# Gated mix of linear attention and expert lookup: output matmuls in a queue, the last tile's scores early, and a new end

## The chip, the core and the metric

The kernel runs on one core of one Trainium2 chip. The metric is device time of one execution in microseconds. A core has five engines that work side by side, each through its own list of instructions in order: TensorE (PE) multiplies matrices into PSUM, VectorE (DVE) and ScalarE (ACT) read and write PSUM and SBUF, GpSimd (POOL) works on SBUF alone, and SyncE (SP) here only issues DMAs. PSUM has eight banks of 512 floats per partition.

## What is computed

The input x has 2048 rows of 512. Two results are mixed by a gate g = sigmoid(x · gate_w): out = g · a + (1 − g) · b.

```python
# a: linear attention with 32 heads of 16
q, k, v = split(x @ wqkv)
phi(t) = concat(softmax(t @ w_phi), softmax(-(t @ w_phi)))
kv, z  = phi(k)^T v,  sum over rows of phi(k)
a      = ((phi(q) kv) / (phi(q) z + 1e-6)) @ wo

# b: 32 heads, each picks one of 16 x 16 experts
s1, s2 = (x w_q)[first half] k1^T, (x w_q)[second half] k2^T
e      = argmax(s1) * 16 + argmax(s2)          # K = 1, so the softmax over K is 1
b      = sum over heads of gelu(x . u[e]) * v[e]
```

Since K is 1, b depends only on how many of the 32 heads pick each expert: b = (count · gelu(x u^T)) v. The count is made with bit operations.

## The kernel before

Rows are cut into 16 tiles of 128. Most products are made in three matmuls per 128 rows of the contraction: every operand is split into a high part (`xh`, `wbh`, `ch`) and a low part (`xl`, `wbl`, `cl`), and high·high, high·low and low·high are added up in one PSUM bank.

The first 130 us form the weights, k, v and the sum kv over all tiles (in the bank `kvacc`). The second part, which the change is about, goes through the tiles again. Its order is written out by hand: the body of a Python loop over `a`, and an end behind it, call helpers, and the order of the calls is the order of the instructions on each engine. Nothing reorders them. In iteration `a` several tiles are under way: n = a+1, a, b = a−1 and z = a−2. The helpers, in the order of one tile's life:

- `front_s(t, half)`: scores of one half, 12 matmuls into a bank `s`. `front_p(t)`: x u^T and the gate, 12 matmuls of 258 columns into `pp`. `best(t, half)` on DVE: maximum and `is_equal` into `eq`. `turn_eq(t)`: a transposing DMA on SP's queue, `eq` to `et`. `gelu_pre(t)` on ACT: what GELU and gate need from `pp`.
- `front_q(t)`: 12 matmuls into `pq`. `soft_in(t)` on DVE: two reductions and two subtractions (`d`); between them stand steps of the count of tile t−1. `soft_exp` on ACT, `soft_w` on POOL (`w`), `soft_sum`, `soft_y`, `soft_p` and `soft_b` on DVE and POOL: the normalised features, again in `d`.
- `mid_mask(t)`: 16 small instructions on PE, `et` to the bank `mk`. `count(t)`: a generator of 18 DVE steps that makes `C`, the count per expert, from `mk`; `step` takes one step, `drain` the rest. Its scratch tiles `sa`, `sb` exist twice, for even and odd t.
- `planes(t)`, `join(t)`: transposition of `d` by ACT copies and two transposing DMAs into `pt`; `mid_phi(t)` does the same with PE transposes and two ACT evictions, without a DMA. `mid_num(t)`: 32 short matmuls into two banks `oT`, ACT writes their high part (`xh`, whose tile is no longer needed), `num_lo(t)` the low part on DVE (`xl`).
- `coef(t)`: count times gelu. `c_planes`, `c_join`, `back_cl`: its transposition by DMA into `ch`, `cl`; `back_c` does it with PE (bank `CT`).
- `back(t)`: 18 output matmuls of 512 columns into one bank `po`: 12 with the attention part (`back_o`, `back_ol`, which want `xh`, `xl`) and 6 with the expert part (`back_out`, which want `ch`, `cl`). `store(t)`: an ACT copy and a DMA.

Four PSUM banks (`mm`) are used in turn by `s`, `pp`, `pq` and `po`, three (`tr`) by `mk`, `oT` and `pt`; `kvacc` has the eighth. In iterations 2 to 9 `back` works on tile z. Iteration 10 makes no output at all (`defer = 10`), and from 11 on `back` is one tile further behind.

Of the kernel before, what the change touches and what calls it, by code (L numbers as in the profile page):

```python
# [20 lines left out]
P = 128  # L21
# [13 lines left out]
def mix_kernel(ctx, tc, xT, wqT, wkT, wv, wphi, wo, wq, kk, ug, ev, cst, out):  # L35
# [6 lines left out]
    def mm_bank(name):  # L42
        return psum.tile([P, 512], F32, tag="mm", bufs=4, name=name)
# [407 lines left out]
    def soft_y(t, i):  # L451
        e = st8[t]
        dve.tensor_reduce(pair(e["st"][:, 224:288])[:, :, 1 - i], hs(e["w"], i), axis=AX.X, op=ALU.add)
# [84 lines left out]
    def mid_mask(t):  # L538
        e = st8[t]
        o = tr_bank(f"mk{t}")[:, :64]  # L540
        for half in range(2):
            for w in range(2):
                for q in range(2):
                    pe.matmul(o[:, half * 32 + w * F:half * 32 + w * F + F], e["et"][:, half * 4 + w * 2 + q, :],
                              wm[:, q, :], start=(q == 0), stop=(q == 1))
        chains[t] = count(t, o)

    def count(t, o):
        e = st8[t]
        A, B = sa[t % 2], sb[t % 2]  # L550
        bor = ALU.bitwise_or
        yield dve.tensor_copy(A[:, :, 8:24], o.rearrange("p (g a) -> p g a", a=F))
        yield dve.tensor_tensor(B[:, :, 8:24], A[:, :, 8:24], A[:, :, 7:23], op=bor)
# [8 lines left out]
        yield dve.tensor_tensor(m2.rearrange("p (w a) -> p w a", a=F), A[:, 2:4, 8:24], A[:, 2:4, 7:23],  # L562
                                op=ALU.bitwise_xor)
# [18 lines left out]
        e["C"] = w3.tile([P, NX], F32, tag="cf", name=f"cf{t}")  # L582
        x8 = X[:, :NX].bitcast(U8).rearrange("p (n b) -> p n b", b=2)
        yield dve.tensor_tensor(e["C"], x8[:, :, 0], x8[:, :, 1], op=ALU.add)

    def coef(t):
        e = st8[t]
        (pool if t < NT - 2 else dve).tensor_tensor(e["C"], e["C"], e["G"], op=ALU.mult)

    def c_planes(t):  # L590
        e = st8[t]
# [26 lines left out]
        ch, cl, o = st8[t]["c"]  # L618
        eng.tensor_tensor(cl, o[:, :2 * P], ch, op=ALU.subtract)

    def back_o(t):
        e = st8[t]
        po = e["po"] = mm_bank(f"po{t}")
        oh, ol, _ = e["o"]
        for k in range(NK):
            pe.matmul(po, oh[:, k, :], wbh[:, k, :], start=(k == 0), stop=False)  # L626
            pe.matmul(po, oh[:, k, :], wbl[:, k, :], start=False, stop=False)  # L627

    def back_ol(t):
        po, (_, ol, _) = st8[t]["po"], st8[t]["o"]  # L630
        for k in range(NK):
            pe.matmul(po, ol[:, k, :], wbh[:, k, :], start=False, stop=False)  # L632

    def back_out(t):
        e = st8[t]
        po = e["po"]
        ch, cl, _ = e["c"]
        for j in range(2):
            js = slice(j * P, (j + 1) * P)
            pe.matmul(po, ch[:, js], eh[:, j, :], start=False, stop=False)  # L640
            pe.matmul(po, ch[:, js], el[:, j, :], start=False, stop=False)  # L641
        for j in range(2):
            pe.matmul(po, cl[:, j * P:(j + 1) * P], eh[:, j, :], start=False, stop=(j == 1))  # L643

    def store(t):
        po = st8.pop(t)["po"]
        ot = w3.tile([P, D], F32, tag="ot", name=f"ot{t}")
        if t < NT - 1:
            act.copy(ot, po)
            sp.dma_start(out[t * P:(t + 1) * P, :], ot)  # L650
        else:
            for i, q in enumerate((sp, act)):
                cols = slice(256 * i, 256 * i + 256)
                (act.copy if i else dve.tensor_copy)(ot[:, cols], po[:, cols])
                q.dma_start(out[t * P:(t + 1) * P, cols], ot[:, cols])
# [59 lines left out]
    def back(t):  # L715
        back_o(t)
        back_ol(t)
        back_out(t)
        store(t)

    defer = 10
    for a in range(NT - 1):
        n, b, z = a + 1, a - 1, a - 2
        y = z if a < defer else -1 if a == defer else z - 1
        B, Z = b >= 0, z >= 0
        if Z:
            mid_num(z)
# [44 lines left out]
        front_s(n, 1)  # L772
        front_p(n, False)
# [34 lines left out]
    back_cl(z, pool)
    num_lo(z)
    for _ in gate(a):  # L810
        step(b)
    step(b, 4)
    soft_in(a)
    soft_exp(a)
    gelu_act(a)
    back(z - 1)
    mid_mask(a)
    soft_w(a)
    gelu_out(a)
# [81 lines left out]
```

## Time and profile before

| | |
|---|---|
| median of 3 runs | 382.03 us (381.43 to 384.12) |
| the profiled execution | 381.71 us, of which its span is 379.9 us |
| PE busy | 367.2 us (97%) |
| DVE busy | 319.9 us (84%) |
| ACT, POOL busy | 236.3 us (62%), 161.3 us (42%) |
| clock of TensorE that was granted | 1.000 |
| second pass over the tiles, from pq of tile 0 | 128.6 us to the end |

Times in the rows below are microseconds from the start of the span; in a timeline row the first number is the start, the second the duration, then engine, line, operation, output, inputs, shapes and count. In the chain of waits each row is one piece of the chain that ended last. Matmuls overlap, so what one costs is the distance to the next start, not its duration. A busy PE is therefore not idle, but it may wait inside for its weights.

### The profile page before, as it was taken

How to read it: one execution, taken by the hardware profiler on the slowest of the kernel's cores; microseconds unless marked ns; L12 is line 12 of the kernel's file. 1: busy time of each engine (PE TensorE's matmuls, PEld its weight loads, DVE VectorE, ACT ScalarE, POOL GpSimd, SP SyncE). 2: the span in 40 equal slices, each digit the busy share in tenths (PEclk: the TensorE clock that was granted, in tenths of full speed). 3: DMA queues.
4: the chain of work that ended last, by engine and by line, in shares of the span. 5: the costliest groups of instructions: out<-in, count | busy, mean ns of one | idle time of the engine just before them, and what ended most of it. 6: DMA issues, size and time to landing. Idle time of an engine off the chain costs nothing.

```text
span 379.9 us, 9164 instructions
## 1 busy us (share of the span) xinstructions
PE 367.2 (97%) x3655; PEld 292.9 (77%) x3655; DVE 319.9 (84%) x785; ACT 236.3 (62%) x416; POOL 161.3 (42%) x170
## 2 busy tenths in 40 slices
PE   7999999999999999999999999999979999999983
PEld 3777687787768888788888888888867878888862
DVE  4459967766868889889999999999999999999993
ACT  4245466546638355869669669668667678678430
POOL 2105445325324733945436436427426436436500
PEclk9999999999999999999999999999999999999999
DMA  7469795596694034254343342342540441441201
GB/s 268 165 239 342 185 288 214 127 272 226 172 307 106 3 85 83 81 74 97 62 95 82 72 97 72 83 98 58 97 98 14 111 99 44 110 90 49 57 31 55
DMA packets 72220, 46.66 MB, mean 123 GB/s; under 512 B 63728, under 2 KB 64496, under 8 KB 69872
## 3 DMA queue, kind: packets, MB, share of 16 engines
q1 hardware_dynamic: 71312, 45.24, 45.2%
q10 hardware_dynamic: 864, 0.82, 0.8%
q8 instruction: 29, 0.48, 0.5%
q14 instruction: 15, 0.12, 0.1%
HBM read 26.39 MB, written 4.19 MB: 80 GB/s over the span
## 4 chain that ended last, share of the span: by engine, by line
PE 45%; DVE 12%; POOL 2%; ACT 2%; issue 1%; ACTq 0%; DVEq 0%
PE s L61 5%; PE s L60 5%; PE s L59 4%; PE pq L61 3%; PE pq L60 3%; PE po L626 3%; PE po L627 3%; PE po L632 3%; PE pq L59 2%; PE oT L525 2%; PE s L57 2%; PE po L640 2%; PE po L643 1%; PE pq L57 1%; PE po L641 1%; PE pp L60 1%
## 5 line engine op out<-in xcount | busy, mean ns | idle before, releaser
L439 POOL TENSOR_TENSOR w<-d,zb 128x512 f32<-128x512 f32 x32 | 40.8, 1296 | 85.3 <-ACT d L433 82.9
L200 POOL TENSOR_TENSOR d<-d,st 128x1024 f32<-128x1024 f32 x16 | 31.1, 1941 | 68.0 <-DVE st L199 58.1
L61 PE MATMUL s<-sh,xl 128*128 128x480 f32 x128 | 48.6, 380 | 0.0
L60 PE MATMUL s<-sl,xh 128*128 128x480 f32 x128 | 48.5, 379 | 0.0
L433 ACT ACTIVATE d<-d 128x512 f32<-128x512 f32 x32 | 20.1, 631 | 45.5 <-DVE d L109 36.8
L474 POOL TENSOR_TENSOR d<-d,st 128x512 f32<-128x512 f32 x30 | 31.2, 1062 | 27.9 <-DVE st L468 25.6
L516 ACT COPY pt<-tp 128x1024 uint16<-128x1024 uint16 x28 | 36.5, 1375 | 0.1
L59 PE MATMUL s<-sh,xh 128*128 128x480 f32 x96 | 36.3, 378 | 0.0
L353 ACT ACTIVATE d<-d 128x1024 f32<-128x1024 f32 x16 | 17.0, 1064 | 26.8 <-DVE d L111 26.7
L506 ACT COPY pl<-d 128x1024 uint16<-128x1024 uint16 x28 | 29.2, 1045 | 5.9 <-POOL d L474 5.9
L61 PEld LDWEIGHTS s<-sh,xl 128*128 128x128 f32 x128 | 24.0, 188 | 4.1
L60 PEld LDWEIGHTS s<-sl,xh 128*128 128x128 f32 x128 | 24.1, 188 | 3.4
L626 PE MATMUL po<-wbh,xh 128*128 128x512 f32 x64 | 25.3, 395 | 0.0
L627 PE MATMUL po<-wbl,xh 128*128 128x512 f32 x64 | 25.1, 392 | 0.0
L198 DVE TENSOR_REDUCE st<-d 128x64 f32<-128x1024 f32 x16 | 19.5, 1219 | 6.4 <-ACT d L353 6.1
L61 PE MATMUL pk<-wah,xl 128*128 128x480 f32 x64 | 24.4, 380 | 0.0
L60 PE MATMUL pk<-wal,xh 128*128 128x480 f32 x64 | 24.3, 380 | 0.0
L60 PE MATMUL pq<-wal,xh 128*128 128x480 f32 x64 | 24.3, 379 | 0.0
L61 PE MATMUL pq<-wah,xl 128*128 128x480 f32 x64 | 24.2, 379 | 0.0
L61 PE MATMUL pv<-wbh,xl 128*128 128x512 f32 x60 | 23.6, 394 | 0.0
L60 PE MATMUL pv<-wbl,xh 128*128 128x512 f32 x60 | 23.5, 392 | 0.0
L483 DVE TENSOR_TENSOR eq<-s,mx 128x512 bf16<-128x512 f32 x32 | 22.1, 692 | 1.2
(176 smaller groups left out, 1053.4 us busy)
## 6 DMA issues: line engine op xcount, KB each, us to landing
wq<-wq SPq DMA_DIRECT2D x16, 1024.0 KB, 5.8
xr<-xT SPq DMA_DIRECT2D x15, 256.0 KB, 6.1
y<-ot SPq DMA_DIRECT2D x15, 256.0 KB, 2.0
rawk<-wkT SPq DMA_DIRECT2D x1, 1024.0 KB, 6.9
rawq<-wqT SPq DMA_DIRECT2D x1, 1024.0 KB, 5.0
rawo<-wo SPq DMA_DIRECT2D x4, 256.0 KB, 3.6
rawu<-ug SPq DMA_DIRECT2D x2, 258.0 KB, 6.3
rawv<-wv ACTq DMA_DIRECT2D x2, 256.0 KB, 4.8
```

Of the source, the lines that this page charges most:

```text
L59: pe.matmul(o_, ah, bh[:, r], start=False, stop=False)
L60: pe.matmul(o_, ah, bl[:, r], start=False, stop=False)
L61: pe.matmul(o_, al, bh[:, r], start=False, stop=(last and i == n - 1))
L200: pool.tensor_tensor(g64(d), g64(d), b64(st[:, 128:192]), op=ALU.mult)
L433: act.activation(hs(d, i), hs(d, i), AF.Exp)
L439: pool.tensor_tensor(hs(e["w"], i), hs(e["ph"], i), hs(zb, i), op=ALU.mult)
L474: eng.tensor_tensor(g64(d)[:, gs_], g64(d)[:, gs_], r[:, gs_].unsqueeze(2).to_broadcast([P, 32, F]), op=ALU.mult)
L483: dve.tensor_tensor(e["eq"][:, 512 * half:512 * half + 512].rearrange("p (h f) -> p h f", f=F), p3, mx.unsqueeze(2).to_broadcast([P, H, F] ...
L506: act.copy(pl, e["ph"][:, halves[i]].bitcast(U16).rearrange("p (c j) -> p j c", j=2))
L516: act.copy(p16[:, :, 4 * i:4 * i + 4, :], e["tp"][i].rearrange("p (j g) n -> p j g n", j=2))
L626: pe.matmul(po, oh[:, k, :], wbh[:, k, :], start=(k == 0), stop=False)
L627: pe.matmul(po, oh[:, k, :], wbl[:, k, :], start=False, stop=False)
```

## The change

Five things are changed.

1. **Output matmuls in a queue.** `push(t)` appends the 18 output matmuls of tile t to a list, `pop(n)` issues the next n. Iteration `a` pushes tile z and pops 17 for a = 3 to 12, else 18, so that one more matmul is left in the list after each of these ten iterations. Even tiles accumulate in the bank of `kvacc`, odd ones in one of the four. `store_ended` copies and stores the tiles whose last matmul was issued. No iteration goes without output matmuls any more.
2. **Tile 15 early.** Scores, `best`, the transposing DMA, the mask and the whole count of tile 15 are made in iteration 1, with a third pair of scratch tiles and a count tile of its own. The mask of tile 1 moves ahead of the scores there. `kv_final` moves ahead of `join(0)`.
3. **The loop ends at iteration 13.** Tiles 14 and 15 have a new end, in which `pp` of tile 15 is made beside tile 14.
4. **In the end**, the features of tile 13 are joined before the exponentials of tile 14; the expert coefficients of tiles 13 and 15 are transposed by DMA, those of tile 14 by PE; `coef` of tile 15 is on POOL.
5. **The output of tile 15** goes into two banks of 256 columns, each with its own 18 matmuls, copy and DMA: expert part first, attention part last.

```diff
 def count(t, o):
-        A, B = sa[t % 2], sb[t % 2]
+        i = 2 if t == NT - 1 else t % 2
+        A, B = sa[i], sb[i]
...
+    def push(t):
+        e, h = st8[t], {}
+        def mm(lhs, rhs, first=False, last=False):
+            def go():
+                if first:
+                    h["po"] = e["po"] = (psum.tile([P, 512], F32, tag="acc", name=f"po{t}") if t % 2 == 0 else
+                                         mm_bank(f"po{t}"))
+                pe.matmul(h["po"], lhs(), rhs, start=first, stop=last)
+                if last:
+                    ended.append(t)
+            return go
...
+    def pop(n):
+        for _ in range(n):
+            queue.pop(0)()
...
-    for a in range(NT - 1):
+    last = NT - 1
+    for a in range(NT - 2):
...
-        if y >= 0:
-            back(y)
-        if a > 1:
+        if Z:
+            push(z)
+            pop(17 if 2 < a < 13 else 18)
+            store_ended()
+        if a > 0:
             mid_mask(a)
...
+        if a == 1:
+            front_s(last, 0)
+            front_s(last, 1)
         if a == 1:
-            mid_mask(a)
             kvacc(NT - 2)
             kvacc(NT - 1)
...
+            best(last, 0)
...
+        if a == 1:
+            best(last, 1)
+            turn_eq(last)
+            front_s(n, 1, range(2))
+            mid_mask(last)
+            front_s(n, 1, range(2, NK))
+            front_p(n, False)
+            kv_final()
...
+        if a == 1:
+            for l in (sa, sb):
+                dve.memset(l[2], 0)
+            drain(last)
...
+    a, b, z = NT - 2, NT - 3, NT - 4
...
+    soft_in(a, dealt(a, b, z))
+    drain(b)
+    gelu_act(a)
+    join(b)
+    push(z)
+    pop(10)
+    mid_mask(a)
+    pop(len(queue))
+    soft_exp(a)
+    store_ended()
+    mid_num(b)
+    front_q(last)
+    soft_w(a)
...
+    gelu_in(last)
+    push(b)
+    pop(12)
+    soft_in(last)
+    soft_exp(last)
+    mid_phi(a)
+    soft_w(last)
+    c_join(b)
+    back_cl(b, pool)
...
+    pop(4)
+    mid_num(a)
+    pop(2)
+    store_ended()
+    num_lo(a)
+    soft_y(last, 0)
...
+    push(a)
+    pop(12)
+    mid_phi(last)
+    c_join(last)
+    back_cl(last, pool)
+    drain(a)
+    coef(a)
...
+    last_c(last, pA, cA)
+    mid_num(last)
+    last_c(last, pB, cB)
+    num_lo(last)
+    back_c(a)
+    back_cl(a)
+    last_o(last, pA, cA)
...
+    pop(6)
+    store_ended()
+    last_o(last, pB, cB)
```

DVE between iterations 1 and 2, before (`sa1`, `sb1` belong to the count of tile 1, `mx1_2` and `eq2` to the best of tile 2, `oT0_0` and `oT1_0` to tile 0, `pq2` to tile 2):

```order
L555 TENSOR_TENSOR sb1_83<-sa1_81 128x4x16
L468 SCALAR_TENSOR_TENSOR st21_1916<-st21_1916,gs1_1857 128x32 x2
L556 TENSOR_TENSOR sa1_81<-sb1_83 128x4x16
L482 TENSOR_REDUCE mx1_2_2112<-s1_2_2039 128x32
L483 TENSOR_TENSOR eq2_2076<-s1_2_2039,mx1_2_2112 128x512
L536 TENSOR_TENSOR xl_62<-oT0_0_2125,xh_61 128x256
L536 TENSOR_TENSOR xl_62<-oT1_0_2126,xh_61 128x256
L105 TENSOR_REDUCE st22_2175<-pq2_2158 128x32
```

The same place after the change; `X15`, `T15` and `cf15` belong to the count of tile 15:

```order
L578 TENSOR_TENSOR X15_2182<-X15_2182,T15_2183 128x512
L579 TENSOR_TENSOR T15_2183<-X15_2182 128x256
L580 TENSOR_SCALAR X15_2182<-T15_2183 128x128
L581 TENSOR_SCALAR T15_2183<-T15_2183 128x128
L582 TENSOR_TENSOR X15_2182<-X15_2182,T15_2183 128x256
L586 TENSOR_TENSOR cf15_2194<-X15_2182 128x256
L536 TENSOR_TENSOR xl_62<-oT0_0_2196,xh_61 128x256
L536 TENSOR_TENSOR xl_62<-oT1_0_2197,xh_61 128x256
L105 TENSOR_REDUCE st22_2246<-pq2_2229 128x32
L397 RECIPROCAL gs2_2163<-gs2_2163 128x1
```

Between the best of tile 2 and the low part of tile 0's result (`xl`) now stands the whole count of tile 15, of which these are the last six steps.

ACT in the end, before, from the join of tile 13's coefficients on (`pt14` are the evictions of tile 14's transposes, `d215` the exponentials of tile 15):

```order
L600 COPY ctj13_4671<-tpc13_4624 128x2x256
L604 CAST ch13_4673<-ctj13_4671 128x256
L499 COPY pt14_4689<-pt0_14_4690 128x512
L499 COPY pt14_4689<-pt1_14_4696 128x512
L433 ACTIVATE d215_4718<-d215_4718 128x32x16 x2
L405 ACTIVATE gs15_4643<-gs15_4643 128x1
```

The same instructions after the change:

```order
L433 ACTIVATE d215_4759<-d215_4759 128x32x16 x2
L499 COPY pt14_4767<-pt0_14_4768 128x512
L499 COPY pt14_4767<-pt1_14_4774 128x512
L602 COPY ctj13_4783<-tpc13_4720 128x2x256
L606 CAST ch13_4785<-ctj13_4783 128x256
L405 ACTIVATE gs15_4734<-gs15_4734 128x1
```

The exponentials of tile 15 have moved from behind `ch13` and `pt14` to ahead of both.

More of the change, by code (lines that the diff above doesn't have):

```diff
@@ L581, in count @@
         yield dve.tensor_tensor(X[:, :NX], X[:, :NX], T[:, :NX], op=ALU.add)
-        e["C"] = w3.tile([P, NX], F32, tag="cf", name=f"cf{t}")
+        e["C"] = (w4.tile([P, NX], F32, tag="cfl", bufs=1, name=f"cf{t}") if t == NT - 1 else
+                  w3.tile([P, NX], F32, tag="cf", name=f"cf{t}"))
         x8 = X[:, :NX].bitcast(U8).rearrange("p (n b) -> p n b", b=2)
@@ L587, in coef @@
         e = st8[t]
-        (pool if t < NT - 2 else dve).tensor_tensor(e["C"], e["C"], e["G"], op=ALU.mult)
+        (dve if t == NT - 2 else pool).tensor_tensor(e["C"], e["C"], e["G"], op=ALU.mult)
     def c_planes(t):
@@ L619, in back_cl @@
         eng.tensor_tensor(cl, o[:, :2 * P], ch, op=ALU.subtract)
[L621 to L624, printed above, removed]
+    queue, ended = [], []
+    def push(t):
[9 more added lines that the diff above has]
+            return go
@@ L625, in back_o @@
         for k in range(NK):
[L626 to L630, printed above, removed]
+            queue.append(mm(lambda k=k: e["o"][0][:, k, :], wbh[:, k, :], first=k == 0))
+            queue.append(mm(lambda k=k: e["o"][0][:, k, :], wbl[:, k, :]))
         for k in range(NK):
-            pe.matmul(po, ol[:, k, :], wbh[:, k, :], start=False, stop=False)
@@ L634, in back_out @@
[L634 to L637, printed above, removed]
+            queue.append(mm(lambda k=k: e["o"][1][:, k, :], wbh[:, k, :]))
+        part = lambda i, j: lambda: e["c"][i][:, j * P:(j + 1) * P]
+        for j in range(2):
+            queue.append(mm(part(0, j), eh[:, j, :]))
+            queue.append(mm(part(0, j), el[:, j, :]))
+        for j in range(2):
+            queue.append(mm(part(1, j), eh[:, j, :], last=j == 1))
+    def pop(n):
+        for _ in range(n):
+            queue.pop(0)()
@@ L638, in back_out, with store_ended, last_c @@
+    def store_ended():
+        for t in ended:
+            ot = w3.tile([P, D], F32, tag="ot", name=f"ot{t}")
+            act.copy(ot, st8.pop(t)["po"])
+            sp.dma_start(out[t * P:(t + 1) * P, :], ot)
+        ended.clear()
+    def last_c(t, po, cols):
+        ch, cl, _ = st8[t]["c"]
         for j in range(2):
             js = slice(j * P, (j + 1) * P)
-            pe.matmul(po, ch[:, js], eh[:, j, :], start=False, stop=False)
-            pe.matmul(po, ch[:, js], el[:, j, :], start=False, stop=False)
+            pe.matmul(po, ch[:, js], eh[:, j, cols], start=(j == 0), stop=False)
+            pe.matmul(po, ch[:, js], el[:, j, cols], start=False, stop=False)
@@ L642, in back_out @@
         for j in range(2):
[L643 to L655, printed above, removed]
+            pe.matmul(po, cl[:, j * P:(j + 1) * P], eh[:, j, cols], start=False, stop=False)
@@ L657, in kv_final, with last_o @@
+    def last_o(t, po, cols):
+        oh, ol, _ = st8[t]["o"]
+        for k in range(NK):
+            pe.matmul(po, oh[:, k, :], wbh[:, k, cols], start=False, stop=False)
+            pe.matmul(po, oh[:, k, :], wbl[:, k, cols], start=False, stop=False)
+        for k in range(NK):
+            pe.matmul(po, ol[:, k, :], wbh[:, k, cols], start=False, stop=(k == NK - 1))
     def kv_final():
@@ L771, in mix_kernel @@
             w4 = ctx.enter_context(tc_pool("w4", "right"))
-        front_s(n, 1)
-        front_p(n, False)
+            for l in (sa, sb):
+                l.append(w4.tile([P, 4, 24], U16, tag=f"s{len(sa)}{len(sb)}", bufs=1, name=f"s{len(sa)}{len(sb)}"))
+        if a > 0:
+            front_s(n, 0)
+        if a != 1:
+            front_s(n, 1)
+            front_p(n, False)
         soft_w(a)
@@ L780, in mix_kernel @@
             wo_load((2, 3))
-        best(n, 0)
+            best(last, 0)
+        else:
+            best(n, 0)
         soft_y(a, 0)
         soft_y(a, 1)
+        if a == 1:
[4 more added lines that the diff above has]
+            front_s(n, 1, range(2, NK))
+            front_p(n, False)
+            kv_final()
         soft_p(a)
@@ L790, in mix_kernel @@
         if a == 1:
-            kv_final()
             for k in range(2, NK):
@@ L797, in mix_kernel @@
                 pool.tensor_tensor(wbl[:, k, :], rawo[k], wbh[:, k, :], op=ALU.subtract)
+            best(n, 0)
         best(n, 1)
@@ L800, in mix_kernel @@
         gelu_pre(n)
-    a, b, z = NT - 1, NT - 2, NT - 3
+        if a == 1:
+            for l in (sa, sb):
+                dve.memset(l[2], 0)
+            drain(last)
+    a, b, z = NT - 2, NT - 3, NT - 4
     mid_num(z)
+    planes(b, 0)
     c_join(z)
+    planes(b, 1)
     front_q(a)
-    mid_phi(b)
+    front_p(last, False)
     gelu_in(a)
-    gelu_out(b)
[L808 to L819, printed above, removed]
+    num_lo(z)
+    soft_in(a, dealt(a, b, z))
[11 more added lines that the diff above has]
+    soft_w(a)
+    gelu_out(b)
+    coef(b)
     soft_sum(a, 0)
     soft_sum(a, 1)
-    mid_num(b)
-    back(z)
     soft_y(a, 0)
-    step(a)
     soft_y(a, 1)
     soft_p(a)
-    soft_b(a, lambda t: None)
+    c_planes(b)
@@ L829, in mix_kernel @@
+    soft_b(a)
+    gelu_pre(last)
     num_lo(b)
-    back_o(b)
-    mid_phi(a)
-    back_ol(b)
-    drain(b)
-    coef(b)
+    for _ in gate(last):
+        pass
+    gelu_in(last)
[3 more added lines that the diff above has]
+    soft_exp(last)
+    mid_phi(a)
+    soft_w(last)
+    c_join(b)
+    back_cl(b, pool)
+    gelu_act(last)
+    gelu_out(last)
+    coef(last)
+    soft_sum(last, 0)
+    soft_sum(last, 1)
+    pop(4)
     mid_num(a)
-    back_c(b)
+    pop(2)
+    store_ended()
     num_lo(a)
-    back_cl(b)
@@ L839, in mix_kernel @@
-    back_out(b)
-    store(b)
+    soft_y(last, 0)
+    soft_y(last, 1)
+    gelu_out(a)
+    c_planes(last)
+    soft_p(last)
+    soft_b(last, lambda t: None)
+    push(a)
[3 more added lines that the diff above has]
+    back_cl(last, pool)
     drain(a)
     coef(a)
-    back_o(a)
-    back_ol(a)
+    poA, poB = mm_bank("poA"), mm_bank("poB")
+    pA, pB = poA[:, :256], poB[:, :256]
+    cA, cB = slice(0, 256), slice(256, 512)
+    last_c(last, pA, cA)
+    mid_num(last)
+    last_c(last, pB, cB)
@@ L845, in mix_kernel @@
+    num_lo(last)
     back_c(a)
     back_cl(a)
-    back_out(a)
-    store(a)
+    last_o(last, pA, cA)
+    ot = w3.tile([P, D], F32, tag="ot", name=f"ot{last}")
+    act.copy(ot[:, cA], pA)
+    sp.dma_start(out[last * P:, cA], ot[:, cA])
+    pop(6)
+    store_ended()
+    last_o(last, pB, cB)
+    otB = w3.tile([P, D], F32, tag="ot", name=f"otB{last}")
+    act.copy(otB[:, cB], pB)
+    act.dma_start(out[last * P:, cB], otB[:, cB])
 def _consts():
```

9 lines of the change are left out of this document (removed).

## The prediction

> **What bounds the kernel now.** I read TensorE's (PE's) own waits first, then the chain of work that ended last, and the timelines around the two places that the change touches. PE's waits (waiter, what released it, us in total, times, longest):
>
> ```profile
> PE CT L611 <- DVE cf L588: 2.4, 2, 1.7
> PE mk L544 <- DMA et<-eq: 2.0, 1, 2.0
> ...
> PE po L640 <- ACT ch L614: 1.0, 2, 0.5
> ...
> PE oT L525 <- ACT kvb L660: 0.8, 1, 0.8
> PE oT L525 <- ACT pt L516: 0.6, 1, 0.6
> ```
>
> From the first tile iteration on, PE idles 6.8 us and no more. 3.4 of it (CT, po) lies at the very end, 2.6 (mk, pt) in iteration 10, where the old kernel leaves one tile's output out, and 0.8 in front of iteration 2. Everything else is PE after PE. One steady iteration in the chain that ended last (start, us, what), with the VectorE (DVE) rows that follow:
>
> ```profile
> 319.48 0.43 PE pq L57
> 322.30 0.23 PE po L626
> ...
> 326.66 0.33 PE s L57
> 333.47 0.60 PE oT L525 x32
> 334.06 0.43 PE pq L57
> 336.92 0.69 DVE st L105
> ...
> 339.47 0.33 DVE cl L619
> ...
> 341.92 0.60 DVE d L109
> ```
>
> An iteration is 14.58 us of PE: pq 2.8, the 18 output matmuls and the mask 4.4 (0.23 for one matmul), scores and pp 6.8, oT 0.6. DVE's own round is in its timeline:
>
> ```profile
> 322.42 0.68 DVE L105 TENSOR_REDUCE st<-pq 128x32 f32<-128x512 f32 x1
> ...
> 336.06 0.75 DVE L536 TENSOR_TENSOR xl<-oT,xh 128x256 fp32r<-128x256 f32 x2
> ```
>
> From pq's first reduction to the end of xl it works without a gap for 13.6 + 0.7 = 14.3 us, then waits 0.2 for the next pq (336.92). The two engines are almost equally loaded: work that is moved from one place to another is free only where it meets an idle.
>
> **Part 1: tile 15's scores, mask and count in iteration 1.** Rows of the old iteration 1, on PE and on DVE:
>
> ```profile
> 149.64 0.40 PE L57 MATMUL s<-sh,xh 128*128 128x512 f32 x1
> ...
> 152.25 0.36 PE L544 MATMUL mk<-wm,et 128*128 128x16 bf16 x8
> 152.54 1.30 PE L207 MATMUL kvacc<-v,d 128*32 128x16 f32 x128
> 153.77 0.50 PE L57 MATMUL s<-sh,xh 128*128 128x512 f32 x1
> ...
> 158.84 1.21 PE L525 MATMUL oT<-pt,kvb 64*32 64x128 f32 x32 [0.78 <-ACT kvb L660]
> ```
> ```profile
> 152.96 0.68 DVE L482 TENSOR_REDUCE mx<-s 128x32 f32<-128x512 f32 x1
> 153.67 0.69 DVE L483 TENSOR_TENSOR eq<-s,mx 128x512 bf16<-128x512 f32 x1
> 154.28 1.27 DVE L453 TENSOR_REDUCE st<-w 128x32 f32<-128x512 f32 x2
> ```
>
> PE: half a score is 149.64 to 152.25, 2.6; mask 0.3; kvacc 1.2. In the new order PE does from 149.64 mask 0.3, scores of 15 5.2, kvacc 1.2, scores of 2 5.2, mask of 15 0.3, pp 1.6: oT can start at 163.4, 4.6 later than 158.84. There the old kernel waited for kvb and ran oT 0.6 longer than in the chain's row; in the new order the kvb copies stand before the join and are long done, so the 0.6 goes: **+4.0** at pq of tile 2, which ends at 163.4 + 0.6 + 2.8 = 166.8. Moved DMAs: the transpose of tile 15's eq goes into SP's queue here, behind two loads of wo; its mask stands six matmuls into s1 of tile 2, and I take it as covered (it costs up to 1 if the transpose is late).
>
> DVE: best of tile 15 is two halves of 1.3 (152.96 to 154.28), and the count is what the old tail shows it to be when nothing is woven into it:
>
> ```profile
> 367.76 0.19 DVE L553 TENSOR_TENSOR sb<-sa 128x64 uint16<-128x64 uint16 x1
> ...
> 372.55 0.42 DVE L584 TENSOR_TENSOR cf<-X 128x256 f32<-128x256 uint8 x1
> ```
>
> That is 5.2 us, 5.6 with the cast and two small memsets. From 152.96: 1.3, sums 1.2, 1.3, the softmax chain 1.5 to 2.2, so about 158.7; then DVE waits for s1 of tile 2, which PE ends at 161.9, best 1.3 (163.4), count 5.6: 169.0. Only behind it stand the low part of o (xl, 0.7) and, 2.9 after pq's first reduction started, cl (336.92 to 339.47 + 0.33): cl of tile 0 is there at 172.6. PE needs it at the 17th output matmul, 166.8 + 16 x 0.23 = 170.5. **+2.0**, a wait of the whole PE queue (mask, scores of tile 3, everything behind), and no later slack gives it back. Its bounds: 0, if DVE's steps are quicker than alone, up to 5.3 by the next rows, POOL and DVE side by side:
>
> ```profile
> 145.34 0.74 POOL L401 TENSOR_TENSOR x<-x,px 128x256 f32<-128x256 f32 x1
> ```
> ```profile
> 145.38 0.73 DVE L562 TENSOR_TENSOR m<-sa 128x32 uint16<-128x32 uint16 x1
> ```
>
> The count's small step started with POOL's product and ended with it: 0.73 for a 32-column step. By the Trainium skill, "SBUF — State Buffer", section "Who interferes with whom", a DVE instruction with two SBUF inputs and a GpSimd instruction that reads SBUF hold a shared port against each other, each for its whole length. The trace agrees in this row, and the rule speaks against moving the count next to POOL's work; by it the sum would go to the slow rival below if POOL's long subtractions were still running.
>
> **Part 2: one matmul put off in each of iterations 3 to 12.** 10 x 0.23 = **-2.3**; DVE's 14.3 just fits under the 14.35 that is left. The old kernel leaves a tile out in iteration 10, and the new one does not. That stretch (from:to, its length, then busy us of PE, PE's loads, DVE, ACT, POOL, clock, DMA):
>
> ```profile
> 276.68:290.02 13.34, 10.82 (x97) 8.75 (x89) 12.59 (x34) 9.22 (x17) 6.74 (x7) 1.00 0.35 70
> ```
>
> 13.34 (10.82 of PE, so 2.5 idle) against 14.58: **+1.2**. The second PSUM bank for the even tiles costs nothing: the four rotating banks are then used by four tiles instead of five. Sum up to pq of tile 14: 4.0 + 2.0 - 2.3 + 1.2 = +4.9, so it starts at 334.06 + 4.9 = 339.0.
>
> **Part 3: the new end.** The old stretch from 334.06 to the end (379.9) is 45.8. Rows of prices, from ScalarE (ACT), POOL and the DMA list, and then the end of the chain:
>
> ```profile
> 337.66 0.78 ACT L600 COPY ctj<-tpc 128x512 uint16<-128x512 uint16 x1 [0.73 <-DMA tpc<-plc]
> 338.46 0.41 ACT L604 CAST ch<-ctj 128x256 fp32r<-128x256 f32 x1
> 338.77 1.04 ACT L506 COPY pl<-d 128x1024 uint16<-128x1024 uint16 x1
> ...
> 344.81 2.61 ACT L516 COPY pt<-tp 128x1024 uint16<-128x1024 uint16 x2
> ...
> 363.97 1.08 ACT L499 COPY pt<-pt 128x512 f32<-128x512 f32 x2 [1.69 <-PE pt L497]
> ```
> ```profile
> 352.69 0.91 POOL L619 TENSOR_TENSOR cl<-ctj,ch 128x256 fp32r<-128x256 f32 x1
> ```
> ```profile
> tp<-pl SPq DMA_TRANSPOSE x28, 3.3
> ```
> ```profile
> 356.37 0.64 ACT d L433
> 357.08 2.56 POOL w L439 x2
> 359.66 0.69 DVE st L453
> ...
> 361.77 1.29 DVE d L474 x2
> ...
> 376.73 0.37 ACT ot L654
> ```
>
> The new end is a chain through all engines. Counted from the start of pq of tile 14 (the old 334.06): the second half of planes of tile 13 starts at +4.7 on ACT and takes 1.0; its transpose lands 3.3 later, +9.0; the join, which now stands **before** the exponentials of tile 14, takes 1.3, +10.3 (the exponentials could have started at +8.5, after d at 342.5). Exponential 0.6, POOL's w 2.6, the sum and softmax chain 2.1 (359.66 to 361.77), 0.5 for steps that meet POOL's next two products: +16.1. xl of tile 13 0.7, three steps of soft_in of tile 15 at 0.6: the exponentials of tile 15 start at +18.6.
>
> Behind these, on ACT in this order: exponentials 1.2, evictions of pt of tile 14 1.1, join and ch of tile 13 1.2: +3.5. PE stands before the four c matmuls of tile 13, which want that ch, and does nothing for some 3.5 us; the transposes of 14 are done, and oT of 14 is behind. Then four matmuls 1.0, oT 0.6, hand-over and xl 1.3 (DVE idles for that, with all of tile 15's sums behind xl): +6.4. Sums of 15 1.2, chain 1.5, scaling 1.3: +10.4. Transposes of 15 and their last eviction 1.2, join and ch of 15 1.2, cl on POOL 0.9: +13.7. Then PE alone: two half matmuls, oT 0.6, six halves 0.8, CT 0.4, twelve halves 1.5, six matmuls 1.4, twelve halves 1.5 (a half costs 0.13, as pp's 12 in 1.6): +20.1. Eviction 0.5, and 2.8 from there to the end of the span, as 377.1 to 379.9 now: **+23.4**. The count of 14 runs beside this and is done in time for CT. Together 18.6 + 23.4 = 42.0, 3.8 less than the old 45.8.
>
> Sum: 339.0 + 42.0 = 381.0 of span against 379.9. The profiled execution took 381.71, 1.8 more than its span, and the median of the runs is 0.3 above it: **383.1 us**. The moved work fills 5.5 us of PE where PE had only 1.4 idle, and what the end gains by it is mostly lost to new waits in the end.
>
> **Rivals.** *PE stays full to the end.* If exponentials and joins come earlier than I reckon, PE's own work from 339.0 counts: pq twice 5.6, pp 1.6, mask 0.3, 64 output matmuls 14.7, oT three times 1.8, pt 1.6, 36 halves 4.7, CT 0.4: 30.7, the end 373.0, the time 375. For it: PE is the bound of every old stretch. Against it: the ACT order above, which no idle of PE can change. 0.20, with the part-way cases up to 378.
>
> *The count of tile 15 meets POOL* (slower). In iterations 1 to 2 POOL has two 128x512 subtractions for wbl (1.3 each, as half of w's 2.6) and a product of 0.7. I have them end when the count begins, near 163.5. If the casts before them are a microsecond or two later, the count is held for up to 3.3, and each 0.1 goes into PE's wait: 386.4. The port page named above is the rule behind this mechanism. 0.14.
>
> *The put-off matmuls shorten nothing*, because another engine holds the iteration at 14.58: +2.3, 385.4. DVE's 14.3 speaks against it. 0.13, half of it slower.
>
> **How the numbers follow.** Forecast 0.53, the three rivals 0.20, 0.14, 0.13. One per cent (about what a measurement of this kernel can tell from no change) is 3.8 us: 378.2 to 385.9. Faster: the first rival, 0.20. Slower: the second, half of the third and the upper end of the forecast's own terms, 0.24. The rest, 0.56, is within one per cent. The forecast's own range is 380 to 386 (2.0 to 0 in iteration 2, a microsecond either way in the end). To hold 8 in 10 it goes on to 377, into the first rival, and 387.5.
>
> **What would show it.** Iteration 2: a PE wait of about 2 us on cl, and DVE without a gap between best of tile 2 and xl. Iterations 3 to 12: 14.35 each from pq to pq. The end: PE waiting some 3.5 us for ch of tile 13, DVE about 3.5 us for xh of tile 14, exponentials of tile 14 behind the join. It is wrong if PE shows less than 5 us of idle after pq of tile 14, or if that pq starts outside 337 to 342.

## The result

The changed kernel takes **385.5 us** (median of 20 runs, 382.95 to 387.58). The kernel before takes 382.04 beside it (median of 20 runs, 381.22 to 385.54). The ratio is **1.0078** with a 95% interval of 1.0058 to 1.0099, so the change costs 2 to 4 us. The forecast was 383.1, with a range of 377.0 to 387.5 and "within one per cent" as the likeliest case. So it came out 2.4 us above the forecast, on the slower side and within one per cent.

The profiled execution of the changed kernel took 385.89 us with a span of 384.1 us, 1.8 apart as before. The forecast span was 381.0, so 3.1 us have to be found. I follow the steps of the prediction through the trace of after.

First TensorE's own waits, as they were read of before (waiter, what released it, us in total, times, longest):

```profile
PE po L633 <- ACT ch L606: 3.0, 1, 3.0
PE poA L665 <- ACT ch L606: 1.8, 1, 1.8
...
PE po L633 <- DVE xl L536: 1.2, 1, 1.2
PE po L633 <- DVE cl L621: 1.0, 1, 1.0
```

The waits of before (CT, mk, kvb, pt, the old ch) are gone, and there are two new places: iteration 2 (xl and cl of tile 0, 2.2 us together) and the end (ch of tile 13, 3.0, and ch of tile 15, 1.8). The forecast had named both places, with 2.0 and 3.5.

**Iterations 1 and 2**, PE's timeline, then DVE's (start, us, what; in brackets the idle before it and what ended that):

```profile
164.04 0.67 PE L525 MATMUL oT<-pt,kvb 64*32 64x128 f32 x32
...
170.58 1.20 PE L633 MATMUL po<-wbh,xl 128*128 128x512 f32 x4 [1.20 <-DVE xl L536]
...
173.69 0.73 PE L633 MATMUL po<-eh,cl 128*128 128x512 f32 x2 [0.98 <-DVE cl L621]
...
181.37 0.67 PE L525 MATMUL oT<-pt,kvb 64*32 64x128 f32 x32
```
```profile
164.19 0.23 DVE L553 CAST s<-mk 128x64 uint16<-128x64 f32 x1
...
165.71 0.94 DVE L571 TENSOR_TENSOR X<-m,m 128x256 uint32<-128x256 uint32 x1
...
170.10 0.75 DVE L536 TENSOR_TENSOR xl<-oT,xh 128x256 fp32r<-128x256 f32 x2
...
173.22 0.42 DVE L621 TENSOR_TENSOR cl<-ctj,ch 128x256 fp32r<-128x256 f32 x1
```

DVE counts tile 15 from 164.2 to 170.1 and only then makes xl and cl of tile 0, and PE stands with its whole queue behind them. From oT of tile 0 to oT of tile 1 it takes 181.37 - 164.04 = 17.33 us.

**The loop**, PE's timeline again:

```profile
281.77 0.67 PE L525 MATMUL oT<-pt,kvb 64*32 64x128 f32 x32
...
296.13 0.67 PE L525 MATMUL oT<-pt,kvb 64*32 64x128 f32 x32
...
340.06 0.50 PE L57 MATMUL pq<-wah,xh 128*128 128x512 f32 x1
```

An iteration takes 14.36 (forecast 14.35). pq of tile 14 starts at 340.06 (forecast 339.0). From there to the end of the span it is 44.0 us (forecast 42.0, before 45.8).

**The end**, ScalarE's timeline, then one row of DVE:

```profile
346.80 2.69 ACT L516 COPY pt<-tp 128x1024 uint16<-128x1024 uint16 x2 [0.85 <-DMA tp<-pl]
349.37 1.15 ACT L433 ACTIVATE d<-d 128x512 f32<-128x512 f32 x2
...
357.98 1.22 ACT L433 ACTIVATE d<-d 128x512 f32<-128x512 f32 x2 [1.90 <-DVE d L109]
359.11 1.05 ACT L499 COPY pt<-pt 128x512 f32<-128x512 f32 x2
...
360.86 0.40 ACT L606 CAST ch<-ctj 128x256 fp32r<-128x256 f32 x1
```
```profile
364.93 0.76 DVE L536 TENSOR_TENSOR xl<-oT,xh 128x256 fp32r<-128x256 f32 x2 [5.01 <-ACT xh L529]
```

The join of tile 13 stands before the exponentials of tile 14. The exponentials of tile 15 start 17.9 after pq of tile 14 (forecast 18.6), and behind them come the evictions of pt, the join and ch, so PE gets ch at 361.3. DVE waits 5.0 for xh of tile 14 (forecast 3.5). From the exponentials of tile 15 to the end of the span it takes 384.1 - 358.0 = 26.1 us, and the forecast had 23.4. **This is the term that is off the most.** What the forecast had not looked at is the granted clock (from:to, length, then busy us of PE, PE's loads, DVE, ACT, POOL, clock, DMA share, GB/s):

```profile
358.30:361.50 3.20, 0.18 (x1) 0.18 (x2) 1.51 (x3) 3.17 (x8) 2.67 (x3) 0.83 0.00 0
361.50:365.40 3.90, 3.90 (x39) 2.48 (x40) 0.47 (x2) 1.42 (x4) 2.72 (x4) 0.50 0.00 0
...
372.30:374.00 1.70, 1.63 (x39) 1.09 (x39) 1.56 (x5) 0.00 (x0) 0.59 (x1) 1.00 0.00 0
374.00:377.50 3.50, 3.50 (x23) 3.50 (x18) 1.86 (x5) 1.02 (x3) 0.00 (x0) 0.51 0.02 5
```

After the 3.0 us wait PE works at half its clock, and shortly after the 1.8 us wait for 3.5 us again. From 377.5 on it is 1.00 again. Theory A is therefore: *the two waits cost their own length and, in addition, the clock behind them.* Theory B: *the end is longer because of hand-overs and shared ports, and the low clock is only the record of an idle engine.*

### The profile page after: what moved, and what is told of

It is laid out like the page before. It is cut to its first block, busy times and chain, and to the rows that moved or that the text cites. A ratio compares the mean times of both kernels' runs of the same rounds, so it can differ in the third digit from the quotient of the medians.

```text
span 384.1 us, 9201 instructions
## 1 busy us (share of the span) xinstructions
PE 371.8 (97%) x3671; PEld 296.6 (77%) x3671; DVE 318.0 (83%) x784; ACT 237.3 (62%) x419; POOL 163.0 (42%) x172
## 4 chain that ended last, share of the span: by engine, by line
PE 43%; DVE 11%; ACT 3%; issue 3%; DMA 2%; POOL 1%; POOLq 0%; ACTq 0%; SPq 0%
PE po L633 11%; PE s L61 5%; PE s L60 5%; PE s L59 4%; PE pq L61 2%; PE pq L60 2%; PE pq L59 2%; PE oT L525 2%; PE s L57 2%; PE pp L60 1%; PE pp L61 1%; PE pq L57 1%; PE pp L59 1%; DMA et<-eq 1%; DVE st L453 1%
## 5 line engine op out<-in xcount | busy, mean ns | idle before, releaser
L633 PE MATMUL po<-wbh,xh 128*128 128x512 f32 x60 | 24.2, 403 | 0.0
L633 PE MATMUL po<-wbl,xh 128*128 128x512 f32 x60 | 24.0, 400 | 0.0
L482 DVE TENSOR_REDUCE mx<-s 128x32 f32<-128x512 f32 x32 | 21.8, 680 | 2.2 <-PE s L61 2.2
```

What stands on the lines that cost most here:

```text
L482: dve.tensor_reduce(mx, p3, axis=AX.X, op=ALU.max)
L633: pe.matmul(h["po"], lhs(), rhs, start=first, stop=last)
```

## The experiments

**1. Both waits filled.** PE gets 12 matmuls that nobody reads before ch of tile 13 is needed, and 7 before ch of tile 15 is.

```diff
+    def fill(n):
+        for _ in range(n):
+            pe.matmul(fb, wbh[:, 0, :P], wbh[:, 1, :], start=True, stop=True)
...
     soft_sum(last, 1)
+    fb = mm_bank("fill")
+    fill(12)
     pop(4)
...
+    fill(7)
     last_c(last, pA, cA)
```

> The changed kernel, with matmuls that nobody reads put into two of PE's waits in the end: 12 of 512 columns between the transposes of tile 14 and the c matmuls of tile 13 (12 x 0.23 = 2.8 of the 3.0 us wait), and 7 (1.6 of 1.8) before the first half matmuls of tile 15. Nothing else waits less. Theory A (the clock): after a wait PE's granted clock is halved for some microseconds, and this made the end 2.7 longer than predicted. Then with PE kept busy the clock stays at 1.00 in all of the end, the four c matmuls and oT of tile 14 take 1.5 instead of 3.0 us (about -1.1 on the chain through xl of tile 14), and the stretch from the halves of poB to the first of poA is 1.6 shorter: 382.8 us, 2.7 under the changed kernel's 385.5, so a ratio of about 1.002 to the kernel before. Theory B (the end is longer because of hand-overs, DVE behind xh and shared ports, and the clock in the records only shows that PE was idle): no change, 385.5 or, if the added matmuls delay ch, up to 386.

Measured: **383.25 us**, ratio to before 1.0021 (1.0004 to 1.0039), profiled span 381.4. The clock in the trace of this run (columns as above), and the start of tile 15's exponentials on ACT:

```profile
361.50:363.00 1.50, 1.50 (x36) 0.89 (x35) 0.00 (x0) 0.78 (x2) 1.12 (x2) 1.00 0.00 0
...
372.00:374.50 2.50, 2.50 (x48) 2.04 (x47) 2.04 (x6) 1.02 (x3) 0.00 (x0) 1.00 0.02 7
```
```profile
357.97 1.23 ACT L433 ACTIVATE d<-d 128x512 f32<-128x512 f32 x2 [1.91 <-DVE d L109]
```

Theory A gave 1.002 and 382.8, theory B 385.5. Doing useless work in the wait makes the kernel 2.3 us faster. The clock stays at 1.00, and from the exponentials of tile 15 to the end of the span it is now 381.4 - 358.0 = 23.4, the forecast's figure. Theory B falls.

**2. Only the first wait filled.** The same without `fill(7)`.

> As the run with both waits filled, but only the first wait (3.0 us, before the c matmuls of tile 13) is filled; the second (1.8 us, before the halves of tile 15) stays. Theory A1: each wait of some 2 us has its own stretch of half clock. Then only the first part of the gain is there, -1.1: 384.4, and the clock still falls to 0.5 between the halves of poB and those of poA. Theory A2: the second stretch is an after-effect of the first (or of the idle summed up over both). Then the clock stays at 1.00 in both and the time is that of both filled, 382.8. Theory B (not the clock): 385.5.

Measured: **384.75 us**, ratio 1.0064 (1.0043 to 1.0085). PE's waits and the clock behind the one that is left:

```profile
PE poA L669 <- ACT ch L606: 1.8, 1, 1.8
```
```profile
372.50:376.00 3.50, 3.50 (x45) 3.12 (x45) 2.04 (x6) 1.02 (x3) 0.00 (x0) 0.53 0.02 5
```

A1 said 384.4, A2 382.8. The second stretch of half clock is there without the first: 1.8 us of waiting is enough here. By the medians, filling the second wait is worth 1.5 us and filling the first 0.7. Only the 1.5 is clear of noise: the interval of this run overlaps that of the changed kernel (1.0058 to 1.0099).

**3. The join of tile 13 ahead of the exponentials of tile 15**, a move that takes the wait itself away.

```diff
     soft_in(last)
+    c_join(b)
     soft_exp(last)
     mid_phi(a)
     soft_w(last)
-    c_join(b)
     back_cl(b, pool)
```

> The changed kernel, with one move in the end: the join and ch of tile 13 stand on ACT before the exponentials of tile 15 and the evictions of pt of tile 14, not behind them. Theory (the order on ACT makes the 3.0 us wait): the transpose of the coefficients of 13 lands near 357.5, join and ch are done at 358.7 instead of 361.3, exponentials start 0.7 later (358.7), pt of 14 is evicted at 361.0. PE waits 0.4 for ch and 1.4 for pt instead of 3.0 in one piece, oT of 14 ends near 361.6 instead of 364.4, and all behind it is 2.5 earlier; if the clock then stays at 1.00 through the end another 1.6 goes: 381.5 (383 if the clock still falls at the second wait). Rival: the softmax of tile 15 through POOL's product w is the chain (exponentials 0.7 later, so w and the sums too): then 386.

Measured: **383.41 us**, ratio 1.0029 (1.0006 to 1.0051). Its waits and a stretch of clock:

```profile
PE poA L665 <- ACT ch L606: 1.8, 1, 1.8
PE po L633 <- POOL cl L621: 1.3, 1, 1.3
```
```profile
361.50:365.40 3.90, 3.23 (x8) 2.56 (x9) 3.65 (x10) 1.54 (x4) 2.73 (x4) 0.64 0.19 69
```

The 3.0 us wait is gone, as the theory has it, and 2.1 us with it. Not 4, because cl of tile 13 still stands behind w on POOL, which makes a new wait of 1.3, and the clock falls once more. The expectation had 383 for a clock that still falls at the second wait. The time fits, but the place does not: in this trace the clock falls behind the new wait of 1.3, and the 1.8 us wait has no half clock behind it.

**4. The count of tile 15 late.** Iteration 1 keeps only the cast of the mask; the rest of the count goes into DVE's 5.0 us gap in the end.

```diff
-            drain(last)
+            step(last)
...
     gelu_out(last)
-    coef(last)
     soft_sum(last, 0)
     soft_sum(last, 1)
+    drain(last)
+    coef(last)
```

> The changed kernel, but of the count of tile 15 only the cast of its mask is done at the end of iteration 1; the rest (5.2 us of DVE) stands in the end, between the sums of tile 15's exponentials and xl of tile 14, where DVE was idle for 5.0 us. Theory: the wait of PE in iteration 2 on xl and cl of tile 0 (2.2 us) goes whole, the rest of the loop keeps 14.36 per iteration, and the end is 0.2 to 0.6 longer (the count ends when xh of tile 14 comes, and a step or two meets POOL): 383.7. Rival: the wait in iteration 2 is only one of several that end together (xl, POOL, the c of tile 0), and 1 us or less of it goes: 384.5 to 385.5. Second rival: the count in the end meets POOL's products w, cl and px, is held for 2 us, and eats the gain: 385.5.

Measured: **385.19 us**, ratio 1.0083 (1.005 to 1.0115). PE's timeline around iteration 2 and DVE's in the end:

```profile
163.69 0.67 PE L525 MATMUL oT<-pt,kvb 64*32 64x128 f32 x32
...
178.28 0.67 PE L525 MATMUL oT<-pt,kvb 64*32 64x128 f32 x32
```
```profile
356.96 1.19 DVE L555 TENSOR_TENSOR s<-s 128x64 uint16<-128x64 uint16 x1
...
359.40 0.96 DVE L571 TENSOR_TENSOR X<-m,m 128x256 uint32<-128x256 uint32 x1
...
363.82 0.75 DVE L536 TENSOR_TENSOR xl<-oT,xh 128x256 fp32r<-128x256 f32 x2
```

Iteration 2 takes 178.28 - 163.69 = 14.59 instead of 17.33: the count in iteration 1 costs **2.74 us** there, and all of it is DVE's. But the end gives most of it back. The count takes from 356.8 to 363.8, 7.0 us instead of the 5.2 it takes alone, since POOL's products w, cl and px run beside it (1.19 for the step at 356.96, which takes 0.19 in iteration 1, and 0.96 for the one at 359.40, which takes 0.43 alone). xl of tile 14 and the sums of tile 15 stand behind it. The profiled end is 45.6 us from pq of tile 14 (382.6 - 337.0) instead of 44.0, and PE has a new wait of 1.9 there, for the scaled features of tile 15. By the medians only 0.3 us of the gain is left, and by the ratios none that can be told from noise. The second rival is the one that happened.

**5. Nothing put off.** `pop(17 if 2 < a < 13 else 18)` becomes `pop(18)`.

> The changed kernel, but every iteration from the third does all 18 output matmuls of its tile; none is put off. Theory: PE sets the iteration, so it takes 14.58 again instead of 14.36, pq of tile 14 starts 10 x 0.23 = 2.3 later (342.4), and as the end behind it hangs on ACT, POOL and DVE, the ten matmuls that are missing there are no gain: 385.5 + 2.3 = 387.8, up to 388.5 if PE's longer idle in the end costs clock. Rival (the put-off matmuls only move work, the end is as much shorter as the loop is longer): 385.5.

Measured: **387.68 us**, ratio 1.0148 (1.0118 to 1.0178), 2.2 above the changed kernel, as the theory said. PE's timeline:

```profile
268.25 0.67 PE L525 MATMUL oT<-pt,kvb 64*32 64x128 f32 x32
...
282.83 0.67 PE L525 MATMUL oT<-pt,kvb 64*32 64x128 f32 x32
```

14.58 per iteration. The ten matmuls that are put off are worth what ten matmuls take, and doing them in the end costs next to nothing: from pq of tile 14 the end takes 43.4 us here against 44.0, since PE waits there anyway.

**6. Ten put off at once.** `pop(8 if a == 2 else 18)`: in iteration 2 PE leaves what needs xl and c, and goes on.

> The changed kernel, but the ten put-off matmuls are put off in one place: iteration 2 does the 8 of tile 0 that need only xh and leaves the 4 on xl and the 6 on c to iteration 3; all later iterations do 18. Theory: the wait of iteration 2 (2.74 us by the run with the count moved, where the iteration took 14.59 instead of 17.33) goes, because PE has the mask and scores to do while DVE finishes the count of tile 15; DVE catches up at 0.28 us per iteration (14.58 less 14.3). pq of tile 14 starts at 337.3, the end is as before: 382.8. Rival: c and po of a tile are now held until the next iteration has begun, the copies that refill them wait, and the loop loses as much: 385 or more.

Measured: **388.7 us**, ratio 1.0177 (1.0154 to 1.02), 3.2 slower instead of 2.7 faster. PE's timeline:

```profile
179.09 0.45 PE L525 MATMUL oT<-pt,kvb 64*32 64x128 f32 x16 [3.16 <-ACT pt L516]
180.30 0.58 PE L525 MATMUL oT<-pt,kvb 64*32 64x128 f32 x16 [0.75 <-ACT pt L516]
180.81 0.80 PE L57 MATMUL pq<-wah,xh 128*128 128x512 f32 x1
```

The wait came back at the next place where DVE is in the chain: pt of tile 1, whose join stands on ACT behind the exponentials of tile 2, which wait for DVE. It is 3.9 us now, half clock follows (0.80 for a first matmul of pq that takes 0.50 in the loop), and the iterations behind it are 14.6 again. The rival had the sign right and the mechanism wrong: no buffer was waited for.

**7. A new order in the end**, same work: the join first as in 3, cl of tile 13 on DVE, the sums of tile 15 ahead of xl of tile 14, oT of tile 15 ahead of its c matmuls, and the xh halves of tile 15 ahead of CT.

```diff
     soft_in(last)
+    c_join(b)
+    back_cl(b)
...
-    c_join(b)
-    back_cl(b, pool)
...
-    num_lo(a)
     soft_y(last, 0)
     soft_y(last, 1)
+    num_lo(a)
...
-    last_c(last, pA, cA)
     mid_num(last)
+    last_c(last, pA, cA)
     last_c(last, pB, cB)
     num_lo(last)
+    last_oh(last, pA, cA)
+    last_oh(last, pB, cB)
     back_c(a)
     back_cl(a)
-    last_o(last, pA, cA)
+    last_ol(last, pA, cA)
```

> The changed kernel with another order in the end alone, same work: join and ch of tile 13 ahead of the exponentials of tile 15 on ACT, cl of tile 13 on DVE instead of behind w on POOL, the sums over w of tile 15 ahead of xl of tile 14 on DVE, oT of tile 15 ahead of its c matmuls, all xh halves of tile 15 ahead of CT. Theory: the three waits of PE that the run with the join moved still shows (0.3, 1.35, 1.8) fall to about 0.3, 0.3 and 1.1 in two pieces; pt of tile 15 starts at 365.5 instead of 369.1, the last eviction is 5 to 6 us earlier, and the clock stays at 1.00 most of the time: 379.5 (378 to 381.5). Rival: the wait only moves on, to oT of tile 15 or to CT behind the count of tile 14 (DVE needs 4.3 for it after the scaling): not below 382.5.

Measured: **380.68 us**, ratio **0.9973 (0.9957 to 0.9989)**: faster than both kernels, 4.8 below the changed one by the medians and 4.0 by the ratios. PE's waits in its end:

```profile
PE poA L665 <- ACT ch L606: 0.7, 1, 0.7
PE pt L497 <- DVE d L474: 0.5, 1, 0.5
...
PE oT L525 <- ACT pt L499: 0.3, 1, 0.3
```
```profile
357.00:366.00 9.00, 7.67 (x65) 5.02 (x63) 8.11 (x19) 5.84 (x13) 6.17 (x7) 1.00 0.16 46
366.00:376.00 10.00, 8.38 (x83) 6.57 (x80) 5.96 (x18) 4.48 (x10) 0.74 (x1) 1.00 0.05 16
```

No wait over 0.7 is left, and the clock never falls. It is a little above the 379.5 expected, and inside its 378 to 381.5.

**8. Runs 6 and 7 together.**

> The new order in the end and the ten matmuls put off at once in iteration 2, together. The two places have nothing in common, so the gains add: 2.7 below the run with the new end alone, 376.8 (375.5 to 379), a ratio of about 0.986 to the kernel before. Rival: what the loop gains is waited for again in the end (the chain through ACT and POOL from tile 13 starts with DVE, which is late): the same as the new end alone.

Measured: **384.69 us**, ratio 1.0081 (1.0056 to 1.0106). From PE's waits:

```profile
PE oT L525 <- ACT pt L516: 3.7, 2, 3.2
```

The new end gives 4.0 here (4.8 alone), and the ten at once cost 4.0 (3.2 in 6): PE waits 3.7 for pt of tile 1. That the two effects add was right to within a microsecond; the sign of one of them was not.

**9. xl and cl of tile 0 ahead of the count**, on top of 7: in iteration 2 `num_lo(0)` and, on POOL, `back_cl(0)` stand before `drain(last)`.

```diff
         if Z:
             num_lo(z)
+        if a == 2:
+            back_cl(z, pool)
+            drain(last)
...
-            if z >= 0:
+            if z > 0:
                 back_cl(z)
...
-            drain(last)
+            step(last)
```

> The kernel with the new order in the end, and in iteration 2 the low part of o of tile 0 on DVE ahead of the count of tile 15, and cl of tile 0 on POOL. So the two products that PE waited for there (1.2 on xl, 1.0 on cl) are early, but DVE has the same work but 0.4, and is as late with the rest of the iteration. Theory (DVE's own load bounds iteration 2, PE's wait is only where it shows): PE's wait moves to oT of tile 1, behind the exponentials and the join, and iteration 2 gets shorter by some 1.2 to 1.6 of its 2.7 surplus only (in the run that put ten matmuls off at once, pq of tile 3 came 1.2 earlier and then waited for pt): 379.2. Rival (the wait was only a matter of order): all of 2.7 goes, 378.0. Second rival: 380.7, nothing gained.

Measured: **383.1 us**, ratio 1.0026 (1.0 to 1.0053), 2.4 slower than 7. DVE's and PE's timelines, and the clock behind PE's wait:

```profile
164.70 0.75 DVE L536 TENSOR_TENSOR xl<-oT,xh 128x256 fp32r<-128x256 f32 x2 [1.43 <-ACT xh L529]
```
```profile
179.85 0.45 PE L525 MATMUL oT<-pt,kvb 64*32 64x128 f32 x16 [2.30 <-ACT pt L516]
```
```profile
181.70:187.00 5.30, 5.30 (x22) 4.47 (x19) 4.22 (x17) 4.38 (x10) 2.78 (x3) 0.73 0.48 84
```

The wait moved to pt of tile 1, as the theory says, but nothing was won. DVE now idles 1.4 for xh before it can begin the count, and the two waits of 1.2 and 1.0 have become one of 2.3 with another 0.75 behind it, after which PE runs at half clock for a while. The clock is not all of it: the two runs of this kernel at 0.998 have spans of 379.5 and 379.9, and those of 7 at 0.999 and above have 378.3 to 379.7. I had priced the moved wait by its length alone, the mistake of the prediction once more.

**10. cl on POOL in every iteration, 18 matmuls put off**, on top of 9: `back_cl(z, pool)` for all tiles of the loop, `pop(16 if 2 < a < 12 else 18)`.

> As the run with xl first, but in every iteration cl is made by POOL instead of DVE (0.73 there, 0.34 less on DVE), and iterations 3 to 11 put off two output matmuls each, 18 in all instead of 10. Theory (the loop's floor of 14.36 is set by two engines that are within 0.1 of each other): with DVE at 13.96, PE at 14.13 sets the iteration: pq to pq 14.13 in iterations 3 to 11, 8 x 0.23 = 1.8 less in all, and the 8 more matmuls in front of pq of tile 15 are done while PE would wait there: 377.4. Rival: POOL's product meets DVE's steps, one of them is held for 0.7 in each iteration, DVE stays at 14.3 and the iteration with it: no gain over the run with xl first, 379.2.

Measured: **384.89 us**, ratio 1.0072 (1.0046 to 1.0097), slower than 9. DVE's timeline over one iteration, and POOL's product beside it:

```profile
202.12 0.68 DVE L105 TENSOR_REDUCE st<-pq 128x32 f32<-128x512 f32 x1
...
203.63 0.79 DVE L574 TENSOR_SCALAR T<-X 128x256 uint32<-128x256 uint32 x1
...
216.56 0.68 DVE L105 TENSOR_REDUCE st<-pq 128x32 f32<-128x512 f32 x1
```
```profile
203.52 0.75 POOL L621 TENSOR_TENSOR cl<-ctj,ch 128x256 fp32r<-128x256 f32 x1 [0.55 <-ACT ch L606]
```

DVE's round is 14.44 us now, longer than the 14.36 it has in run 9 with cl on it: a step that takes 0.29 is held to 0.79 by the product that was taken off DVE. PE has two matmuls fewer than 18 and waits instead: from one oT to the first matmul of pq it is 0.87 here (at 212.4) and 0.60 in run 9, because pt comes late. So the rival's mechanism holds, though not its time of 379.2, and DVE, not PE, sets this loop.

## Why the prediction was right, and where it was not

**The loop.** Part 1's first term (oT of tile 0 at 163.4, no wait for kvb) came out at 164.04 without one. Its second, the wait in iteration 2, was 2.0 in the forecast, all of it on cl; PE's waits show 2.2, of which 1.2 is on xl, and run 4 prices the whole at 2.74. In its working for DVE, best of tile 2 ends at 163.4, where its own terms give 163.2; it ended at 164.1. Part 2's -2.3 is confirmed by the row (14.36) and by the undoing (run 5, +2.2). Together pq of tile 14 came 1.1 later than forecast, 0.6 from oT of tile 0 and 0.7 from iteration 2, less 0.2 of small differences.

**The end.** The chain to the exponentials of tile 15 took 17.9 instead of 18.6, with the join of 13 ahead of the exponentials of 14 as said. The step that failed is the one from there, "+23.4": it took 26.1. Its list of work was right, since with the waits filled (run 1) the same list took 23.4, and so were the stops on the way: there xl of tile 14 ends at +6.4, the scaling at +10.3, cl at +13.6 and PE's last matmul at +20.3, where the forecast had +6.4, +10.4, +13.7 and +20.1. In the changed kernel xl ends at +7.7, cl at +14.9 and the last matmul at +22.9, so 1.3 of the 2.7 comes before xl and 1.4 behind cl, at the two stretches of half clock. What failed is its prices: it took every matmul behind the two waits at rows measured at full clock, though the same step had PE do nothing for "some 3.5 us" ahead of them. The one row of before that it quotes with an idle PE (13.34 us, 2.5 of them idle) shows a clock of 1.00, so that row alone gave no warning; the term needed a bound from above for the clock and had none. By the Trainium skill, "TensorE: Matmul & The Clock Gate", section "HAM oscillation — how this bites in real kernels", TensorE should not be left idle for longer than about 3.4 us, or it falls back to half clock; the price here agrees in kind, but 1.8 us were enough in run 2.

So the time is 2.4 above the forecast: +1.1 from the loop, +2.7 from the clock, -0.7 from the chain, and -0.7 from the step between the profiled execution and the median, which the forecast had put at +0.3 and which is -0.4 here (385.5 against 385.89). The two misses are 3.8 together; that the time stayed within one per cent, 0.4 us inside the bound of 385.9, is owed in part to the two unrelated terms of -0.7. Of the signs of being wrong, pq of tile 14 is inside 337 to 342. PE's idle there is 8.0 us with the time behind its last matmul and 4.8 in the two waits alone, at the edge of the 5 that the prediction asked for.

**The rivals.** *PE stays full to the end* (375): no. Run 7, with another order on all engines, comes 4.8 of the 10.5 us from the measured 385.5 towards it, part of them by the clock. *The count of tile 15 meets POOL* (386.4): one step did, 0.94 instead of 0.43 at 165.71, so 0.5 and not 3.3; the long subtractions ended at 164.0. Where the count was moved to the end (run 4) it met w, cl and px and took 1.8 longer. *The put-off matmuls shorten nothing* (385.4): refuted by the row of 14.36 and by run 5. That the times of these two rivals lie nearer to the measured one than the forecast does is a coincidence.

**Why the change is no gain.** It moves 5.5 us of PE's work and 5.2 us of DVE's out of the end. DVE's part comes back as 2.74 us in iteration 2, and the three other orders of runs 6, 9 and 10 did not recover that, as DVE is the engine that is late. The end became 1.8 shorter, and 5.3 more lay in it: run 7 does the same work in another order in 38.7 us from pq of tile 14 (378.9 - 340.2) instead of 44.0. About half of that is the clock, by the 2.7 of run 1.

## What to carry to other kernels

Price a wait of TensorE by its length and, where some 1.5 us of idle or more come together within 3.4 us, bound it from above by one or two stretches of 3.4 us at half clock behind it (an estimate from that length: up to 1.7 us are lost in each). Idle in pieces of up to 0.7 us cost no clock in run 7, and a row of useless matmuls tells in one run whether the clock is what a stretch suffers from. When a wait is taken away, ask which engine was late: where it was the releaser's own load (runs 6 and 9), the wait came back at the next thing that this engine's work led to, and in a longer piece.

## What the runs showed of the hardware

The clock fell after less idling than I would have thought, and its switches look like a grid. In the profiled execution of the changed kernel, half clock begins near 360.4 (0.83 over 358.3 to 361.5 is 1.1 us of half clock, put at the end of that stretch), ends at 367.1, begins at 374.0 and ends at 377.5: 6.7, 6.9 and 3.5 apart, two, two and one times about 3.4 to 3.5. The Trainium skill, "TensorE: Matmul & The Clock Gate", section "What's actually happening", has a window of 3413 ns that runs freely, and the distances agree with it. It has the clock fall after at least one idle window; with such a grid the windows that end at 360.4 and at 374.0 held some 2.1 and 1.5 us of idle.

The other traces bear the grid out, though no run was made to test it. In runs 2 to 6 and 8 to 10 every stretch of half clock before the end of the span lasts 3.4 or 6.8 us, and the switches within one trace lie whole multiples of 3.41 us apart; in run 6 this holds even for the 181 us between its first stretch and its second. So what a wait costs depends on where it falls. Run 5, laid over the grid of its own trace (columns as above):

```profile
358.00:361.40 3.40, 1.83 (x12) 1.17 (x10) 3.30 (x6) 1.70 (x4) 2.88 (x4) 1.00 0.14 28
361.40:364.80 3.40, 1.76 (x37) 1.11 (x37) 0.24 (x1) 2.57 (x6) 2.89 (x4) 1.00 0.00 0
368.20:371.60 3.40, 1.41 (x9) 0.84 (x8) 3.19 (x11) 1.40 (x3) 0.00 (x0) 1.00 0.11 22
371.60:378.40 6.80, 5.88 (x53) 5.27 (x54) 4.50 (x12) 1.86 (x5) 0.73 (x1) 0.50 0.01 2
```

Its wait of 3.1 us for ch of tile 13 is split over the first two windows, 1.6 us of idle in each, and the clock stays at 1.00. The third holds 2.0 us of idle, made of two waits, and 6.8 us of half clock follow. In run 3 two waits of 0.3 and 1.3 in one window bring the clock down, and the 1.8 us wait, split over two, does not. Over the second pass in these traces, a window at full clock with less than 1.5 us of idle was never followed by half clock, one with more than 1.8 always was, and between the two both happened. What decides there is not shown.

A grid that runs freely would also make the cost differ from run to run, and it does. The 20 runs of the changed kernel have mean granted clocks of 0.987 to 0.996, and its two runs at 0.996 have spans of 381.2, 0.2 above the forecast's 381.0, against 382.9 to 385.8 for the rest. The kernel before has it too: in the 32 runs beside experiments 1 to 4 its spans are 379.0 to 380.0 at a clock of 1.000, and 380.9 to 382.9 at 0.991 and below. With both waits filled all 12 runs were at 0.999 or 1.000.
